# Attention plus gated MLP on one core: head quads outside, query chunks inside, and an exp on VectorE as four shifted bit lines

## The chip, the cores and the metric

The kernel runs on one core of a Trainium2 chip. The metric is the time of one execution in device microseconds (us). Both kernels were run several times on the same chip in alternation, and every run quoted here as a comparison is of the state "fast" unless the text says otherwise. The engines are TensorE (PE in the profile, PEld for its weight loads), VectorE (DVE), ScalarE (ACT), GpSimd (POOL) and SyncE (SP, which issues most DMA). The "granted clock" is the share of full speed that TensorE was given; in the mean of 0.859 of the kernel before, 294 of its 1038 us ran at 0.5 and the others at 1.0 (the first 26 us have no record).

## The reference

For x of 2048 x 640, in bf16:

```python
g = sigmoid((x * gate_w).sum(-1))            # one gate per token
q, k, v = split(x @ wqkv)                    # 32 heads of 20
a = softmax(q @ k.T * 20**-0.5) @ v @ wo     # full attention, no mask
h = x @ w1 + b1                              # 640 -> 1536
b = (h * tanh(log1p(exp(h)))) @ w2           # mish, 1536 -> 640
out = g * a + (1 - g) * b
```

The cost is dominated by softmax. There are 32 heads x 2048 x 2048 scores, 134 million exps. The kernel computes scores transposed: a block is 128 keys (partitions) x 512 queries of one head. A *group* is four heads with one chunk of 512 queries. There are 32 groups, each with 16 key tiles x 4 heads = 64 blocks, 2048 blocks in all.

## The kernel before

Four engines work on a block. TensorE makes the scores of four heads in four row strips of its array (contraction 20, padded to 32). ScalarE takes three or two blocks per activation out of the score banks and writes exp to bf16. TensorE multiplies with V in four column strips ("PV"), accumulating 32 columns per head in one PSUM bank, where the 21st is the softmax denominator. Some key tiles go to VectorE instead, which builds exp by hand. A small list scheduler inside the kernel fixes the instruction order of each engine when the program is built.

```python
DVE_KEYS = (6, 10, 14)            # 3 of 16 key tiles on VectorE, 13 on ScalarE
...
def ex(...):                      # ScalarE: one exp over 3 or 2 blocks
    nc.scalar.activation(eb.tile[:, 0:w], sb.tile[:, 0:w], ACT.Exp, bias=lnc, scale=inv)
...
# VectorE: bits of 2**y as a line, then power of two, mantissa, square, product
nc.vector.tensor_scalar(out=vb_.tile[...], in0=db.tile, scalar1=P * LOG2E * inv,
                        scalar2=127.0 * P, op0=ALU.mult, op1=ALU.add)       # x4, one per head
nc.vector.tensor_scalar(out=nb_.tile, in0=vb_.tile, scalar1=0xFF80, ... bitwise_and)
nc.vector.tensor_scalar(out=mb_.tile, in0=vb_.tile, scalar1=0x7F, scalar2=0x3F80, ... and, or)
nc.vector.tensor_tensor(out=m, in0=m, in1=m, op=ALU.mult)                   # x2 halves
nc.vector.tensor_tensor(out=m, in0=m, in1=e, op=ALU.mult)                   # x2 halves
pv_four(G, j, 1, ...); pv_four(G, j, 0, ...); pv_four(G, j, 2, ...)         # three V copies, one per coefficient
...
for i, func in enumerate((ACT.Exp, ACT.Ln, ACT.Tanh)):                      # mish, on ScalarE
    ...
ld_wk0 = load(nc.sync, ...); ld_wq0 = load(nc.scalar, ...)                  # small weights first
for c in range(4): ld_x.append(load((nc.sync, nc.scalar)[c % 2], ...))      # then x
ld_wv = load(nc.scalar, ...); ld_gw = load(nc.scalar, ...)                  # on ScalarE's queue too
```

The projections and the MLP use the whole 128 x 128 array (full mode). The group order is query chunk outside, four heads inside, so the output projection of a chunk can run as soon as its eight groups are done.

The softmax here doesn't subtract the row's maximum and nothing guards it: scores larger than these inputs give would overflow.

## Time and profile before

| | before |
|---|---|
| time, median (lowest to highest) of 4 runs | 1041.86 us (1031.25 to 1044.37) |
| span of the profiled run | 1038.2 us |
| ScalarE busy | 921.6 us (89%) |
| TensorE / VectorE busy | 831.3 / 790.8 us |
| mean granted clock of TensorE | 0.859 |
| first exp starts / last exp ends | 27.4 / 1015.5 us |

The profile page gives the busy time of each engine (part 1) and the span in 40 slices (part 2, where 9 means 90% or more):

```profile
PE 831.3 (80%) x6247; PEld 267.3 (26%) x6304; DVE 790.8 (76%) x1322; ACT 921.6 (89%) x731; POOL 35.3 (3%) x29
...
ACT  1757879998999999999999999999999999999991
...
PEclk9998999886696779997789989787989997599766
```

ScalarE is full from about the seventh slice to the last but one. The page's groups, costliest first (busy us, mean ns of one | idle before them and who ended it):

```profile
L597 ACT ACTIVATE E<-S,lnc 128x1536 bf16<-128x1536 f32 (+1 forms) x666 | 822.4, 1357 | 72.5 <-PE C L507 41.9
L579 PE MATMUL S<-q,kt_all 32*128 32x512 bf16 x1664 | 290.5, 428 | 146.1 <-ACT E L597 139.7
...
L663 DVE TENSOR_TENSOR m<-m 128x1024 bf16<-128x1024 bf16 x192 | 127.2, 683 | 0.3
...
L658 DVE TENSOR_SCALAR m<-e 128x2048 uint16<-128x2048 uint16 x96 | 66.2, 690 | 6.6 <-PE C L507 4.0
```

The exps take 822.4 us, 1.235 us each, and wait only 72.5. TensorE waits 139.7 us for ScalarE to free the score banks. So ScalarE bounds the kernel. The last two lines matter for the change: one VectorE operation with a constant does 2048 columns in 690 ns, one with two tensors only 1024 columns in 683 ns.

Who waited for whom (us in total, times, longest us):

```profile
PE S L579 <- ACT E L597: 139.7, 179, 6.2
...
ACT E L597 <- PE C L507: 41.9, 19, 16.1
...
ACT L382 <- DMA w2k<-in_gate_w_dram: 19.2, 1, 19.2
```

The chain of work that ended last, as shares of the span:

```profile
ACT 49%; PE 28%; issue 11%; DVE 7%; DMA 4%; SPq 1%; ACTq 0%; DVEq 0%
```

### The profile page before, as it was taken

The page shows a single profiled execution, that of the slowest core. Times are in us where ns is not written, and L with a number is a line of the kernel's source. Part 1 is how long each engine was busy: PE and PEld are TensorE (multiplying, and loading weights), DVE is VectorE, ACT ScalarE, POOL GpSimd, SP SyncE. Part 2 cuts the span into 40 slices and gives each one's busy share as a digit, 9 for nine tenths or more (in the row PEclk, how much of TensorE's full clock was granted, in tenths as well). Part 3 has the DMA queues.
Part 4 walks back from the last instruction along what each step waited for, and adds up shares of the span by engine and source line. Part 5 has one row for each costly group of instructions (what it writes and reads, how often), then busy time and mean ns, then how long its engine had stood idle before and what let it go on. Part 6 is the DMA issues. An engine that isn't in the chain of part 4 may idle for free.

```text
span 1038.2 us, 15472 instructions
## 1 busy us (share of the span) xinstructions
PE 831.3 (80%) x6247; PEld 267.3 (26%) x6304; DVE 790.8 (76%) x1322; ACT 921.6 (89%) x731; POOL 35.3 (3%) x29
## 2 busy tenths in 40 slices
PE   2899988887886589996689889667988967798885
PEld 1432222221121123321123322112322311132213
DVE  1698989887784769995679879677888975689772
ACT  1757879998999999999999999999999999999991
POOL 9300000000000000000000000000000000000000
PEclk9998999886696779997789989787989997599766
DMA  7400000011000000000000000000000000000001
GB/s 196 109 1 12 12 11 11 12 55 36 9 12 11 11 1 12 25 24 12 11 1 12 18 25 18 12 12 1 12 12 25 24 12 11 1 12 12 11 11 37
DMA packets 28495, 22.36 MB, mean 22 GB/s; under 512 B 15496, under 2 KB 23688, under 8 KB 28424
## 3 DMA queue, kind: packets, MB, share of 16 engines
q1 hardware_dynamic: 24744, 19.15, 6.7%
q10 hardware_dynamic: 3680, 2.23, 0.8%
q8 instruction: 49, 0.80, 0.3%
q14 instruction: 22, 0.18, 0.1%
HBM read 18.22 MB, written 2.88 MB: 20 GB/s over the span
## 4 chain that ended last, share of the span: by engine, by line
ACT 49%; PE 28%; issue 11%; DVE 7%; DMA 4%; SPq 1%; ACTq 0%; DVEq 0%
ACT E L597 40%; PE S L579 8%; PE C L507 7%; ACT arena L745 6%; PE X L763 3%; PE X L778 3%; PE X L427 2%; DVE e L646 2%; ACT L745 2%; PE X L439 2%; DMA rbc<-rows 2%; PE X L462 2%; PE X L727 1%; DMA w2k<-in_A_wqkv_dram 1%; ACT L597 1%
## 5 line engine op out<-in xcount | busy, mean ns | idle before, releaser
L597 ACT ACTIVATE E<-S,lnc 128x1536 bf16<-128x1536 f32 (+1 forms) x666 | 822.4, 1357 | 72.5 <-PE C L507 41.9
L579 PE MATMUL S<-q,kt_all 32*128 32x512 bf16 x1664 | 290.5, 428 | 146.1 <-ACT E L597 139.7
L646 DVE TENSOR_SCALAR e<-X 128x512 uint16<-128x512 f32 x384 | 260.8, 687 | 135.7 <-PE X L634 131.8
L507 PE MATMUL C<-E,va 128*32 128x512 bf16 x1664 | 183.3, 438 | 2.7 <-DVE oraw L690 1.5
L579 PEld LDWEIGHTS <-kt_all 32*128 32x128 bf16 x1664 | 83.4, 92 | 382.7 <-issue 375.6
L634 PE MATMUL X<-q,kt_all 32*128 32x512 bf16 x384 | 156.1, 428 | 3.6 <-DVE e L646 3.3
L663 DVE TENSOR_TENSOR m<-m 128x1024 bf16<-128x1024 bf16 x192 | 127.2, 683 | 0.3
L668 DVE TENSOR_TENSOR m<-m,e 128x1024 bf16<-128x1024 bf16 x192 | 126.6, 681 | 0.0
L507 PEld LDWEIGHTS <-va 128*32 128x32 bf16 x1664 | 42.5, 95 | 129.4 <-issue 127.4
L727 PE MATMUL X<-xt,w 128*128 128x512 bf16 x219 | 70.5, 416 | 2.5 <-issue 1.7
L658 DVE TENSOR_SCALAR m<-e 128x2048 uint16<-128x2048 uint16 x96 | 66.2, 690 | 6.6 <-PE C L507 4.0
L763 PE MATMUL X<-w2k,arena 128*128 128x320 bf16 x384 | 69.6, 305 | 0.7 <-DVE e L646 0.7
L745 ACT ACTIVATE arena<-arena 128x2048 bf16<-128x2048 bf16 x36 | 68.2, 1917 | 0.2
L653 DVE TENSOR_SCALAR n<-e 128x2048 uint16<-128x2048 uint16 x96 | 65.8, 685 | 0.0
L778 PE MATMUL X<-wo,arena 128*128 128x320 bf16 x256 | 49.3, 325 | 7.8 <-DVE arena L717 6.5
L507 PE MATMUL C<-e,vd 128*32 128x512 bf16 x384 | 49.5, 442 | 4.1 <-DVE e L646 2.2
L507 PE MATMUL C<-m,vd 128*32 128x512 bf16 x384 | 49.1, 452 | 4.2 <-DVE m L668 4.2
L439 PE MATMUL X<-xt,wq 128*128 128x512 bf16 x137 | 48.6, 446 | 2.3 <-issue 1.8
L733 DVE TENSOR_SCALAR arena<-X,b 128x512 bf16<-128x512 f32 x48 | 35.8, 746 | 18.7 <-PE X L727 18.5
L507 PEld LDWEIGHTS <-vd 128*32 128x32 bf16 x1152 | 34.6, 99 | 57.7 <-issue 51.6
L507 PE MATMUL C<-n,vd 128*32 128x512 bf16 x384 | 42.7, 432 | 5.7 <-DVE n L653 5.5
L427 PE MATMUL X<-xt,w2k 128*128 128x512 bf16 x147 | 44.2, 403 | 2.4 <-issue 1.1
(55 smaller groups left out, 435.7 us busy)
## 6 DMA issues: line engine op xcount, KB each, us to landing
rbc<-rows SPq DMA_DIRECT2D x128, 64.0 KB
out_dram<-arena SPq DMA_DIRECT2D x16, 160.0 KB
w<-in_B_w_dram SPq DMA_DIRECT2D x1, 1920.0 KB
w2k<-in_B_w_dram SPq DMA_DIRECT2D x1, 1920.0 KB
arena<-in_A_wqkv_dram SPq DMA_DIRECT2D x2, 700.0 KB
arena<-in_A_x_dram ACTq DMA_DIRECT2D x2, 640.0 KB
arena<-in_A_x_dram SPq DMA_DIRECT2D x2, 640.0 KB
wo<-in_A_wo_dram SPq DMA_DIRECT2D x4, 200.0 KB
```

The costliest lines, as they stand in the source:

```text
L439: nc.tensor.matmul(t[:, 0:QC], lhsT=wq[:, p, k, :], rhs=xt[:, qc, k, :], start=a, stop=b)
L507: nc.tensor.matmul(acc[32 * r:32 * r + 32, :], lhsT=ten[:, off:off + 32], rhs=srcs[r](), start=k == 0, stop=k == pv_per - 1, tile_position ...
L579: nc.tensor.matmul(sb.tile[:, a * QC:(a + 1) * QC], lhsT=kt_all[32 * r:32 * r + 32, G % NP, j * P:(j + 1) * P], rhs=q_buf[G].tile[32 * r:3 ...
L597: nc.scalar.activation(eb.tile[:, 0:w], sb.tile[:, 0:w], ACT.Exp, bias=lnc, scale=inv)
L634: nc.tensor.matmul(db.tile[:, :], lhsT=kt_all[32 * r:32 * r + 32, G % NP, j * P:(j + 1) * P], rhs=q_buf[G].tile[32 * r:32 * r + 32, :], st ...
L646: nc.vector.tensor_scalar(out=vb_.tile[:, r * QC:(r + 1) * QC], in0=db.tile[:, :], scalar1=P * LOG2E * inv, scalar2=127.0 * P, op0=ALU.mul ...
L663: nc.vector.tensor_tensor(out=m, in0=m, in1=m, op=ALU.mult)
L668: nc.vector.tensor_tensor(out=m, in0=m, in1=e, op=ALU.mult)
L727: nc.tensor.matmul(t[:, 0:QC], lhsT=w1[:, k, ft * P:(ft + 1) * P], rhs=xt[:, c, k, :], start=a, stop=b)
L745: nc.scalar.activation(v, hs[:, 4 * a:4 * a + 4, :] if func == ACT.Exp else v, func, bias=1.0 if func == ACT.Ln else 0.0)
L763: nc.tensor.matmul(t[:, 0:320], lhsT=hs[:, k, u * P:(u + 1) * P], rhs=w2[:, k, 320 * hf:320 * hf + 320], start=a, stop=b)
L778: nc.tensor.matmul(t[:, 0:320], lhsT=otn[:, (c * NP + k) % NO, u * P:(u + 1) * P], rhs=wo[:, k, 320 * hf:320 * hf + 320], start=a, stop=b)
```

## The change

The change rewrites the body of the kernel. Its parts, with the lines that carry them:

```diff
-DVE_KEYS = (6, 10, 14)                      # 3 of 16 key tiles on VectorE
+SHIFTS = (0, 19, 51, 90); SUM = 5.2566
+def dve_keys(G): n = 4; ...                 # 4 of 16
 ...
-opn (and), opm (and, or), sq x2, p3 x2; V copies for three coefficients
+nc.vector.tensor_scalar(out=bufs[i].tile[...], in0=bufs[0].tile[...],
+                        scalar1=float(SHIFTS[i]), scalar2=None, op0=ALU.add)   # i = 1, 2, 3
+# PV: the four lines are summed by TensorE with the same V
 ...
-qc, p = divmod(G, NP)                       # query chunk outside
+p, qc = divmod(G, NQ)                       # head quad outside
 ...
-nc.tensor.matmul(t[:, 0:QC], lhsT=w1[:, k, ft * P:(ft + 1) * P], rhs=..., ...)
+for r in range(4):                          # projections, MLP: four column strips
+    nc.tensor.matmul(t[32 * r:32 * r + 32, 0:width], lhsT=lhsT(r), rhs=rhs, ...,
+                     tile_position=(0, 32 * r))
 ...
+if i == 1 and a == 0:
+    nc.scalar.preload_act_table_set("natural_log_exp_and_others")  # exp and ln in one set
 ...
-x after the small weights; padding of weights by GpSimd; wv and gate_w on ScalarE's queue
+x first; no padding; wv and gate_w on SyncE's queue
 ...
+place(): four DMA copies per group pack the heads into 120- and 80-row tiles (6 steps, not 8)
```

The scores times 128 log2(e) plus 127 x 128, stored as an integer and read as bf16, give a piecewise linear picture of exp. The sum of four such lines with shifted bits is smoother, and the common factor 5.2566 goes into ScalarE's exps as a bias. Both schedulers try to let VectorE's score matmuls ride in the unused row strips of ScalarE's score passes. In the traces (matmuls that start within 0.06 us of each other counted as one step) 331 of 384 ride so in the kernel before. The changed kernel begins with 20 matmuls on TensorE whose result is thrown away.

Intent: less work for ScalarE, paid with a cheaper exp on VectorE and some more PV on TensorE.

## The prediction

> **What bounds it now.** ScalarE. On the page of before (span 1038.2 us) ScalarE is busy 921.6 (89%), TensorE 831.3, VectorE 790.8. In the 900-1000 us window ScalarE is busy 96.4 with 80 exps (1.21 us each; groups: 1571 and 1144 ns by form, overlapping their neighbours). Sum: 666 exps x 1.22 = 813 us, 36 mish activations 68, 25 table loads x 1.28 = 32, waits before exps 72.5, start (first exp at 27.4 us), tail 22.7 after the last exp. Of the waits, 23.8 are three stalls on PV matmuls before 110 us.
>
> **What the change does.**
> 1. VectorE takes 4 of 16 key tiles instead of 3; ScalarE keeps 1536 score blocks of 1664: 615 exps instead of 666 (instruction order). 51 x 1.22 = -62 us.
> 2. Table loads fall from 25 to 9: -20 us (1.28 us each here, no visible pause around them).
> 3. VectorE: before, a batch of four blocks is 4x687 + 690 + 685 + 4x682 = 6.85 us; after, 4x687 + 3x690 = 4.82, as the shifts have the form of the 690 ns operation. [...] 128 batches cost 617 us against 658. Starts stand 0.60 apart for 0.69 recorded, so VectorE needs about 730-770 us in all.
> 4. TensorE: PV groups rise from 704 to 896 (x 0.23 = +44 us); output projection from 256 to 192 steps (-9). Row visits stay about 620, but mode switches fall from 1496 to 1290. [...] group starts are 0.23 apart within a mode, 0.32-0.33 across. So -206 x 0.1 = -20 us. Net +15: about 700 us at full clock, an estimate, 780-800 at the granted 0.86.
> 5. GpSimd's padding goes; x loads before weights. First exp near 15 us instead of 27; early stalls shrink by about 10. Tail: one more copy (+2.5), fewer steps (-2).
>
> **Critical path.** Nearly all of 1, 2 and 5 lies on ScalarE's chain: -62 -20 -12 -10 = -104. TensorE and VectorE come close: per group of four heads and 512 queries I estimate ScalarE 26, TensorE 25, VectorE 23 us, so a few more waits, with four exp buffers instead of five.
> Sum: start 15 + early stalls 15 + exps 750 + mish 68 + loads 12 + other waits 45 + tail 24 = 929.
>
> **Predicted: 930 us**, range 890 to 985. Faster by over 2%: 0.92; within: 0.05; slower: 0.03.
>
> **What would show it.** Groups: 615 exps, about 760 us busy; ScalarE above 88%; shifts near 690 ns, VectorE about 770 us; windows: exps every 1.22 us in the middle; first exp near 15 us; PV step still 0.23; granted clock 0.86 or higher [...].
>
> **What would make it wrong.** Column tiles of 320 columns must be issued as eight instructions in 0.14 us; no trace here shows such a rate (PV: eight in 0.23). [...] The fixed instruction order may stall ScalarE where real times differ; output projections all fall into the last groups and may lengthen the end. If VectorE's score waits feed back through the two shared X banks, gaps reach 80 us.

The sum came to 929 us. The costs it uses are those of the trace of the kernel before: 690 ns for a VectorE operation with a constant on 2048 columns, 683 ns for one with two tensors on 1024, 0.23 us from one PV group to the next and 0.32 to 0.33 across a mode switch. The 0.14 us for a step of 320 columns is measured there too: at full clock its full-array matmuls of 320 columns start 0.14 to 0.15 us apart (448 of them).

## The result, and the profile after

The changed kernel took 943.79 us (median of 4 runs, 942.05 to 946.2), against 1041.86 us. The ratio is 0.9078, 95% interval 0.9011 to 0.9145. (Ratios here are the mean time of one kernel's fast runs over that of the other's of the same rounds, so not quite the ratio of the medians.) The prediction was 930 with a range of 890 to 985.

The page of the changed kernel, parts 1, 2 and 4:

```profile
PE 854.3 (91%) x10616; PEld 306.1 (33%) x10616; DVE 755.0 (80%) x1225; ACT 842.2 (89%) x663; POOL 5.5 (1%) x7
...
PEclk9999986699999975999999669999985799867997
...
PE 59%; ACT 22%; DVE 11%; issue 5%; DMA 2%; SPq 1%; ACTq 0%; DVEq 0%
```

The chain has gone over from ScalarE (49% to 22%) to TensorE (28% to 59%), and TensorE is busy 91% of the span. Read alone, this says that TensorE is the bound now. The experiments below ask whether that is so. The groups:

```profile
L627 ACT ACTIVATE E<-S,lnc 128x1536 bf16<-128x1536 f32 x615 | 767.1, 1332 | 63.4 <-PE C L588 40.9
L661 DVE TENSOR_SCALAR t<-X 128x512 uint16<-128x512 f32 x512 | 346.8, 688 | 108.5 <-PE X L600 99.5
L600 PE MATMUL S<-q,kt 20*128 20x512 bf16 x1536 | 259.3, 414 | 43.8 <-ACT E L627 40.6
L674 DVE TENSOR_SCALAR t<-t 128x2048 uint16<-128x2048 uint16 x384 | 252.4, 683 | 3.5 <-PE C L588 1.6
```

There are 615 exps instead of 666, and TensorE waits 40.6 us for ScalarE where it waited 139.7. The sum over ScalarE, from the two groups tables and the order of its instructions in time:

| piece of ScalarE's line | before | after | difference |
|---|---|---|---|
| until the first exp | 27.4 | 11.9 | -15.5 |
| exps, busy | 822.4 | 767.1 | -55.3 |
| table loads (25, 9) x 1.283 | 32.1 | 11.5 | -20.5 |
| mish activations | 68.2 | 69.0 | +0.8 |
| waits just before exps | 72.5 | 63.4 | -9.1 |
| from the last exp to the end | 22.7 | 27.4 | +4.7 |

The differences add up to -94.9 us; the spans differ by 96.4 us (1038.2 to 941.8). The pieces overlap by a few us (the first exp's wait is in two rows, neighbouring groups overlap), which is what is left.

The end got longer. The changed kernel's last 30 us in order of time (start, duration, what, idle before):

```profile
908.83 5.56 ACT L627 ACTIVATE E<-S,lnc 128x1536 bf16<-128x1536 f32 x5 [0.22 <-PE C L588]
...
915.21 5.82 PE L407 MATMUL X<-wo,oc 120*32 120x320 bf16 x164
...
925.07 0.69 DVE L732 TENSOR_TENSOR on<-oraw,rbc 128x512 bf16<-128x512 f32 x1 [4.13 <-DMA rbc<-rows]
925.79 3.05 SPq L741 DMA_DIRECT2D oc<-on  x4
930.15 7.93 PE L407 MATMUL X<-wo,oc 80*32 80x320 bf16 x172 [9.12 <-DMA oc<-on]
```

The denominators travel through DMA as before, then come four new copies (925.79 to 930.15, 4.4 us), then 43 steps of output projection. The line of 915.21 also answers a doubt of the prediction: 164 matmuls are 41 steps of four column strips, 5.82 / 41 = 0.142 us a step at full clock (1.00 from 915.2 to 921.1 us). Four narrow matmuls of 320 columns with their weight loads are issued in that time, which is the rate that the prediction had seen in no trace.

### The profile page after: what moved, and what is told of

Same layout as the page of the kernel before. It is cut to its first block, busy times and chain, and to the rows that moved or that the text cites. A ratio compares the mean times of both kernels' runs of the same rounds, so it can differ in the third digit from the quotient of the medians.

```text
span 941.8 us, 24292 instructions
## 1 busy us (share of the span) xinstructions
PE 854.3 (91%) x10616; PEld 306.1 (33%) x10616; DVE 755.0 (80%) x1225; ACT 842.2 (89%) x663; POOL 5.5 (1%) x7
## 3 DMA queue, kind: packets, MB, share of 16 engines
q8 instruction: 83, 1.36, 0.6%
## 4 chain that ended last, share of the span: by engine, by line
PE 59%; ACT 22%; DVE 11%; issue 5%; DMA 2%; SPq 1%; ACTq 0%; DVEq 0%
ACT E L627 20%; PE C L588 18%; PE S L600 15%; PE X L407 13%; DVE t L661 5%; PE X L600 4%; PE X L479 3%; PE X L462 3%; PE X L498 2%; DVE t L674 2%; ACT arena L771 1%; DMA rbc<-rows 1%; DVE arena L757 1%; SPq L727 1%; DVE on L732 1%
## 5 line engine op out<-in xcount | busy, mean ns | idle before, releaser
L627 ACT ACTIVATE E<-S,lnc 128x1536 bf16<-128x1536 f32 x615 | 767.1, 1332 | 63.4 <-PE C L588 40.9
L661 DVE TENSOR_SCALAR t<-X 128x512 uint16<-128x512 f32 x512 | 346.8, 688 | 108.5 <-PE X L600 99.5
L600 PE MATMUL S<-q,kt 20*128 20x512 bf16 x1536 | 259.3, 414 | 43.8 <-ACT E L627 40.6
L674 DVE TENSOR_SCALAR t<-t 128x2048 uint16<-128x2048 uint16 x384 | 252.4, 683 | 3.5 <-PE C L588 1.6
L588 PE MATMUL C<-t,va 128*32 128x512 bf16 x2048 | 208.1, 421 | 8.1 <-DVE t L674 4.7
L600 PE MATMUL X<-q,kt 20*128 20x512 bf16 x512 | 200.8, 413 | 5.8 <-DVE t L661 4.1
L600 PEld LDWEIGHTS <-kt 20*128 20x128 bf16 x2048 | 79.0, 92 | 295.3 <-issue 286.2
L407 PE MATMUL X<-w,arena 128*32 128x320 bf16 x1536 | 78.9, 308 | 3.3 <-DVE t L661 2.5
L407 PE MATMUL X<-xt,w 128*32 128x512 bf16 x960 | 76.2, 383 | 4.3 <-DVE arena L757 1.9
L479 PE MATMUL X<-xt,wqk 128*32 128x512 bf16 x560 | 49.5, 429 | 0.5 <-DVE t L661 0.5
L462 PE MATMUL X<-xt,wqk 128*32 128x512 bf16 x560 | 44.5, 402 | 0.5 <-DVE t L661 0.5
```

What stands on the lines that cost most here:

```text
L407: nc.tensor.matmul(t[32 * r:32 * r + 32, 0:width], lhsT=lhsT(r), rhs=rhs, start=a, stop=b, tile_position=(0, 32 * r))
L462: nc.tensor.matmul(t[32 * r:32 * r + 32, 0:QC], lhsT=w, rhs=xt[:, sc, k, :], start=k == 0, stop=k == KT - 1, tile_position=(0, 32 * r))
L479: nc.tensor.matmul(t[32 * r:32 * r + 32, 0:QC], lhsT=w, rhs=xt[:, qc, k, :], start=k == 0, stop=k == KT - 1, tile_position=(0, 32 * r))
L588: nc.tensor.matmul(acc[G][32 * r:32 * r + 32, :], lhsT=va4[:, (p // 2) % 2, j, h * VW:h * VW + 32], rhs=buf.tile.bitcast(BF16)[:, off * QC ...
L600: nc.tensor.matmul(t[:, off * QC:(off + 1) * QC], lhsT=kt[32 * r:32 * r + DH, (p % 2) * S + j * P:(p % 2) * S + (j + 1) * P], rhs=q_buf[G] ...
L627: nc.scalar.activation(eb.tile[:, 0:w * QC], sb.tile[:, 0:w * QC], ACT.Exp, bias=lnc, scale=inv)
```

## The experiments

Twelve kernels ran, four to a chip. The kernel before was run on each of the chips (medians 1038.5, 1040.6 and 1040.4 us). The changed kernel itself was not run again there, so differences to its 943.8 us carry the difference between chips, which for the kernel before is 0.3%. In the table, the clock is the range of mean granted clocks over the fast runs; the medians count every run, also one slow run of keys3 and three of best, the ratios only fast ones.

| run | what | time, us (median) | ratio to before, 95% | clock |
|---|---|---|---|---|
| (changed) | | 943.79 | 0.9078 [0.9011, 0.9145] | 0.887-0.900 |
| keys3 | 3 key tiles on VectorE | 1009.70 | 0.9690 [0.9598, 0.9782] | 0.822-0.837 |
| keys5 | 5 key tiles | 1132.73 | 1.0904 [1.0831, 1.0977] | 0.817-0.836 |
| pvless | TensorE -59 us, rescheduled | 966.21 | 0.9293 [0.9238, 0.9348] | 0.831-0.840 |
| pvsame | TensorE -59 us, same order | 956.22 | 0.9196 [0.9167, 0.9224] | 0.835-0.843 |
| htwice | TensorE +52 us | 955.98 | 0.9189 [0.9138, 0.9241] | 0.925-0.937 |
| oldcost | VectorE's exp at the old cost | 1214.02 | 1.1658 [1.1636, 1.1680] | 0.755-0.761 |
| fullmode | MLP, output projection in full mode | 939.28 | 0.9025 [0.8981, 0.9068] | 0.898-0.915 |
| spread | mish spread in time | 947.19 | 0.9114 [0.9077, 0.9152] | 0.892-0.905 |
| tail | shorter end | 936.99 | 0.9011 [0.8977, 0.9045] | 0.885-0.908 |
| best | fullmode + spread + tail | 970.03 | 0.9232 [0.9182, 0.9283] | 0.869-0.879 |
| tablesonly | kernel before + one table set | 1014.27 | 0.9753 [0.9715, 0.9792] | 0.856-0.867 |
| xfirst | kernel before + x first | 1035.09 | 0.9960 [0.9909, 1.0011] | 0.860-0.869 |

Theory S says that ScalarE's line of exps still bounds the kernel. The rival, theory T, says that TensorE does, as the chain and its 91% suggest.

### keys3 and keys5: move key tiles between ScalarE and VectorE

```diff
 def dve_keys(G):
-    n = 4
+    n = 3        # keys3;  n = 5 in keys5
```

> The changed kernel with 3 of 16 key tiles on VectorE instead of 4: 666 exps on ScalarE instead of 615, 800 PV groups instead of 896. Theory S (ScalarE's chain bounds): 51 exps x 1.247 us (767.1 busy over 615) = +64, a little back from waits: 985 to 1005 us. Theory T (TensorE, 91% busy, bounds now): 96 PV groups x 0.23 less, so 920 to 945 us.

> The changed kernel with 5 of 16 key tiles on VectorE: 563 exps (-52 x 1.247 = -65 us of ScalarE), 96 PV groups more (+22 us of TensorE at full clock), 32 more batches on VectorE (32 x (4 x 0.605 + 3 x 0.61) = +136 us, so about 890 busy). Theory S alone: 880 to 900 us. If VectorE or TensorE is the next limit close behind: 945 to 990 us, with ScalarE's busy share down to about 80%.

The run keys3 took 1006.9 us in the mean of its three fast runs (the median above counts a slow one of 1021 us too), 63 us more, although TensorE had 96 PV groups less to do. That is just above the range of theory S (985 to 1005), and against theory T, which had it faster. The clock fell too (0.835 for 0.893 in the profiled runs), so it could be a rival cause. The sum over ScalarE leaves no room for it. The page of keys3:

```profile
PE 863.9 (86%) x10232; PEld 298.1 (30%) x10232; DVE 622.3 (62%) x1001; ACT 905.7 (90%) x714; POOL 5.5 (1%) x7
...
L627 ACT ACTIVATE E<-S,lnc 128x1536 bf16<-128x1536 f32 (+1 forms) x666 | 831.0, 1335 | 64.2 <-PE C L588 39.1
```

ScalarE's busy time rose by 63.5 us (842.2 to 905.7), its waits before exps stayed (63.4 and 64.2), and the span rose by 62.2 (941.8 to 1004.0).

The run keys5 took 1132.7 us, slower than the kernel before, and far past both expectations. ScalarE needed only 711.0 us for its 563 exps, but waited; the same line of the waits, first for the changed kernel, then for keys5:

```profile
ACT E L627 <- PE C L588: 40.9, 52, 3.9
```

```profile
ACT E L627 <- PE C L588: 220.5, 115, 10.8
```

An exp that waits for PV waits for one of the four buffers that PV has to free. VectorE was busy only 889 us (78%), TensorE 1030 us (91%). A first reading is that the PV matmuls stand in a fixed order on TensorE, the bit lines among them, so that everything behind stands still when VectorE's lines come late. TensorE's own waits speak against that as the whole cause. The longest that it spent on VectorE's exp in keys5:

```profile
PE X L600 <- DVE t L661: 11.5, 43, 0.5
PE C L588 <- DVE t L674: 7.5, 12, 2.6
```

All such waits come to about 32 us (19 in the changed kernel). A rival is that TensorE has more to do: only 150 of VectorE's 640 score matmuls ride with ScalarE's, so that all scores take 1074 steps instead of 826. At the 0.23 us of a step at full clock that is 57 us more, an estimate, on top of 22 us of PV. The lower clock (0.828) is not the whole cause either: at full clock too ScalarE was idle for 159 of 710 us, against 34 of 711 in the changed kernel (from the first exp to the last, by the trace's clock records). None of this was tested by itself, so why keys5 lost 190 us stays open.

### oldcost: the fourth tile with the old exp's cost

```diff
-    nc.vector.tensor_scalar(out=t_i, in0=t0, scalar1=SHIFTS[i], op0=ALU.add)
+    for _ in range(2):       # the same operation twice: same result
+        nc.vector.tensor_scalar(out=t_i, in0=t0, scalar1=SHIFTS[i], op0=ALU.add)
```

> Each of the three shift operations on VectorE is done twice, which leaves the result right and gives a batch of four blocks 4 x 0.687 + 6 x 0.683 = 6.85 us, what the old exp cost. VectorE: 755 + 128 x 3 x 0.61 = 989 us busy. If the cheap exp is what makes the fourth key tile affordable: VectorE becomes the bound, 1030 to 1080 us, no better than the kernel before. If VectorE has room for it: below 980 us.

It took 1214 us: in this design the fourth key tile is affordable only because the exp became cheap. The size was again missed by more than 130 us, in the same way as in keys5: VectorE was busy 1008.5 us (83%), as expected, and the exps waited 264.5 us for PV. Here too few of VectorE's score matmuls ride (160 of 512). Both runs say that this design does not degrade gently when VectorE gets more to do.

### pvless, pvsame and htwice: take work from TensorE, or add some

```diff
 # pvless, pvsame: PV of two of the four bit lines is not issued (wrong result on purpose)
-    for items in d_items[G]:
-        pv_four(G, items)
+    for i, items in enumerate(d_items[G]):
+        pv_four(G, items, skip=i % 4 > 1)     # pvsame: the scheduler still counts 228 ns
 # htwice: the first MLP matmul is done twice, the sum starting anew
-    KT, 219, mm,
+    2 * KT, 219, mm,                           # k = k % KT
```

> Wrong result on purpose: the PV matmuls of two of the four bit lines are left out, VectorE still makes all four. TensorE loses 256 groups x 0.23 = 59 us at full clock, ScalarE and VectorE lose nothing. Theory S: only part of the 57 us of waits on TensorE goes, 915 to 935 us. Theory T: 885 to 900 us.

> The first MLP matmul is done twice (the accumulation starts anew, the result is right): 240 column groups more, +52 us of TensorE at full clock, nothing more on ScalarE or VectorE. Theory S: TensorE has some room, 950 to 970 us. Theory T: the whole cost shows, 995 us or more.

> Wrong result on purpose, as pvless (two of four bit lines are not multiplied with V), but with every other TensorE instruction in exactly the order of the changed kernel (9592 of 9592 in place), as the scheduler is told the old cost. The run pvless took 59 us of work from TensorE and came out slower (966 us, clock 0.836). Theory O (the other order that the scheduler chose was to blame): 915 to 940 us, clock about 0.89. Theory C (TensorE's granted clock follows its own activity, so work taken away is paid back as half clock): clock 0.80 to 0.86, 945 to 970 us.

Theory C of pvsame is a guess, drawn from the clocks of pvless (0.836) and htwice (0.925) against 0.893 in the changed kernel. The run pvless was expected to be faster than the changed kernel under both theories, and was 22 us slower. Its clock had fallen from 0.89 to 0.84, and the scheduler had also chosen another order, so pvsame was made to tell the two apart: the order of the remaining 9592 matmuls was exactly that of the changed kernel. It took 956 us, 12 us more than the changed kernel with 59 us of TensorE work less (256 groups x 0.23, an estimate), at a clock of 0.84. So the other order may account for the further 10 us of pvless's loss, not for all of it. The intervals of the ratios of pvsame and of the changed kernel lie close (0.9167 to 0.9224, and 0.9011 to 0.9145), but do not overlap, and the clocks are far apart. In the other direction, htwice (ordered anew) added 52 us of work (240 column groups, an estimate; two such groups take 0.44 us, from 129.26 to 129.70, in the changed kernel), cost 12 us, which lies in the range of theory S, and its clock went up to 0.93.

Where the time went is seen by stages. First the changed kernel, then pvsame, in three windows: length; busy us (instructions) of PE, PEld, DVE, ACT, POOL; granted clock; DMA share and rate:

```profile
200.00:300.00 100.00, 95.69 (x1357) 35.08 (x1354) 87.98 (x144) 95.80 (x79) 0.00 (x0) 1.00 0.07 16
...
700.00:800.00 100.00, 88.98 (x1130) 30.23 (x1123) 76.36 (x122) 94.89 (x75) 0.00 (x0) 0.82 0.06 15
800.00:900.00 100.00, 89.60 (x1013) 28.29 (x1010) 79.80 (x134) 90.80 (x73) 0.00 (x0) 0.83 0.08 21
```

```profile
200.00:300.00 100.00, 93.03 (x1259) 33.26 (x1258) 86.93 (x142) 95.12 (x78) 0.00 (x0) 0.98 0.06 16
...
700.00:800.00 100.00, 85.28 (x980) 27.17 (x977) 76.41 (x123) 95.53 (x74) 0.00 (x0) 0.78 0.05 12
800.00:900.00 100.00, 91.47 (x783) 23.98 (x781) 71.61 (x117) 81.79 (x66) 0.00 (x0) 0.61 0.07 20
```

In the stage at full or nearly full clock (200 to 300 us) both do the same number of activations, 79 and 78, so the TensorE work that pvsame leaves out is worth nothing there: ScalarE is the limit. By 900 us pvsame is 13 activations behind. It lost seven of them in the last of these windows, where its clock is 0.61 instead of 0.83 and ScalarE does 66 instead of 73, and four before 100 us, where its clock was lower too (0.91 for 0.98 from 25 to 100 us).

The sum over all stretches says the same. From the first exp to the last, by the trace's clock records, ScalarE was idle for 34 of 711 us at full clock and 29 of 191 us at half clock in the changed kernel, and for 28 of 612 and 52 of 307 us in pvsame. So pvsame's profiled span, longer by 17.7 us (959.5 for 941.8), has 23 us more of idle ScalarE at half clock and 6 us less at full clock. At full clock the share of idle time is the same (4.8% and 4.5%) with and without the 59 us of TensorE work, so ScalarE is the limit there, which is theory S; but with little to spare, for in htwice it was idle for 50 of 783 us (6.4%). At half clock TensorE more often makes it wait, which is theory T, though not throughout. In this stretch of the changed kernel ScalarE was full, with mish and exps, and TensorE was not:

```profile
167.00:177.00 10.00, 6.67 (x58) 1.95 (x62) 6.82 (x10) 9.99 (x8) 0.00 (x0) 0.54 0.02 2
```

The clock records of the traces hold only 1.0 and 0.5, in stretches that are, but for the ends, multiples of 3.41 us: at half clock from 3.41 to 27.31 us long in the changed kernel and in the kernel before (202 us of the span at half clock in the changed kernel, 294 in the kernel before, 317 in pvsame). No record stands before 9 us in the changed kernel, and before 26 us in the kernel before; the mean clocks count that time as full. With 59 us less TensorE work the clock was lower (pvsame, 0.84 for 0.89), with 52 us more it was higher (htwice, 0.93). But it was also halved without an idle TensorE. This is the changed kernel around one loss of the clock:

```profile
122.00:129.00 7.00, 6.51 (x89) 2.16 (x85) 6.23 (x11) 6.82 (x6) 0.00 (x0) 1.00 0.01 4
129.00:136.00 7.00, 5.76 (x66) 2.40 (x64) 6.65 (x11) 7.00 (x6) 0.00 (x0) 0.95 0.01 1
136.00:143.00 7.00, 6.76 (x49) 1.42 (x46) 4.04 (x9) 5.41 (x4) 0.00 (x0) 0.50 0.17 41
143.00:150.00 7.00, 6.60 (x39) 1.48 (x35) 3.88 (x7) 6.08 (x5) 0.00 (x0) 0.50 0.05 12
```

TensorE was busy 5.76 of 7 us before it lost half its clock, and 6.76 of 7 after, with fewer instructions (49 and 39, for 66). No wait of TensorE in 129 to 136 us was longer than 0.71 us.

That time goes with the clock is also seen without any edit: within one and the same kernel the slower runs mostly had the lower clock. In fullmode the four runs were 934.0, 938.3, 940.3 and 945.4 us at 0.915, 0.907, 0.905 and 0.898; in pvless and htwice, with four runs each, time and clock have a correlation of -0.97. It is negative in every kernel run here, but from -0.60 to -0.99, and the slope is no constant: about 7 us per 0.01 of clock in fullmode (11.3 us over 0.017), 2.4 in tail. A correlation doesn't tell what drives what. The edit of pvsame changed TensorE's work alone, and both clock and time moved.

Nor does the amount of work alone set the clock: keys5, with 22 us more of it (96 groups x 0.23, an estimate), had a lower clock as well (0.817 to 0.836), and oldcost, with the same matmuls, the lowest (0.755 to 0.761). Both spread the work over a longer time (1132.7 and 1214.0 us).

### spread: is it the crowding of mish that costs the clock?

ScalarE's mish operations come in bursts, in which TensorE gets fewer score banks to fill (24 exps in the 49.4 us from 128.6 to 178.0 of the changed kernel, 79 in the 100 us from 200 to 300). In the four stretches of the changed kernel with mish (128.6 to 178.0, 315.8 to 363.6, 498.3 to 544.5 and 682.4 to 732.1 us) the granted clock was 0.65, 0.75, 0.82 and 0.70, against 0.893 over the span. The guess, theory C below, was that spreading them would keep the clock up.

```diff
-    after=at(group + 0.45 * i + 0.12 * a)
+    after=at(group + (1.2 + 0.9 * a, 1.5 + 0.9 * a, 3.5 + 0.5 * a)[i])   # exp, ln, tanh
-    mish(c, base + 3.1)
+    mish(c, base)
```

> The changed kernel with the nine mish activations of each chunk spread over 3.3 groups instead of 1.4 (exp and ln between the softmax exps, tanh later), nothing else. Theory C (half clock comes where mish crowds out the exps and TensorE runs thin): granted clock 0.91 to 0.95 instead of 0.89, waits of the exps down, 930 to 940 us. If the half clock has another cause: clock 0.88 to 0.90, 940 to 950 us.

The clock stayed at 0.892 to 0.905 and the time at 947.2 us. The guess fell. (The edit also shifted the second MLP matmul a little, 4.8 + 1.8 for 4.6 + 2.0 in the code, so "nothing else" is not quite so.) What exactly makes the clock drop stays open.

### fullmode: undo the column tiles of MLP and output projection

```diff
-    for r in range(4):
-        nc.tensor.matmul(t[32 * r:32 * r + 32, 0:width], lhsT=lhsT(r), rhs=rhs, ..., tile_position=(0, 32 * r))
+    nc.tensor.matmul(t[:, 0:width], lhsT=lhsT, rhs=rhs, ...)    # and mode="full" for the scheduler
```

> Undoes the column tiles of the MLP and the output projection alone: each step is one 128-wide matmul in full mode. TensorE's mode switches rise from 1290 to 1447, at 0.1 us each +16 us of TensorE; 2448 fewer matmuls. Theory S: mostly hidden, 943 to 955 us. Theory T: 955 to 970 us. If issuing four narrow matmuls costs time that one wide one does not, it comes out faster, below 940 us.

939.3 us, ratio 0.9025 [0.8981, 0.9068] against 0.9078 [0.9011, 0.9145] of the changed kernel: no loss, perhaps a small gain. (The median lies just under the 940 us of the third expectation, but the runs reach from 934 to 945.) The column tiles of these parts brought nothing, though 157 mode switches came back (1290 to 1447). The prediction had costed the fewer switches at 0.1 us each. A switch does cost that on TensorE; a stretch of the kernel before shows it:

```profile
500.43 0.40 PE L507 MATMUL C<-E,va 128*32 128x512 bf16 x4
500.66 0.39 PE L507 MATMUL C<-n,vd 128*32 128x512 bf16 x4
501.00 0.40 PE L579 MATMUL S<-q,kt_all 32*128 32x512 bf16 x3
...
501.33 0.40 PE L507 MATMUL C<-E,va 128*32 128x512 bf16 x4
```

Starts are 0.23 us apart within the column mode, and 0.34 and 0.33 where column strips give way to row strips and back. But 16 us of that (157 x 0.1, an estimate), in the engine that is not the limit in the full-clock stages, did not show in the time. Some of it may be hidden, as the run also has 2448 matmuls fewer and a slightly higher clock (0.898 to 0.915, for 0.887 to 0.900). Loads of 128x32 weights take 95 to 102 ns in the profiles of the kernel before and of the changed one, those of 128x128 weights 97 to 110 (147 for the first twenty of the changed kernel).

### tablesonly and xfirst: two parts alone, in the kernel before

```diff
 # tablesonly
+    if func == ACT.Ln and a == 0:
+        nc.scalar.preload_act_table_set("natural_log_exp_and_others")
 # xfirst: in the order of the changed kernel
+    x0a = load_x(nc.scalar, 0, 2); x0b = load_x(nc.sync, 2, 4)
     ld_wk0 = ...; ld_wq0 = ...
```

> The kernel before with one part of the change alone: the table set that has exp and ln both is loaded ahead of ln, so that 9 table loads are left of 25. 16 x 1.28 = 20.5 us less on ScalarE. Theory S: ratio 0.98 to the kernel before, 1015 to 1025 us. If these loads stood in ScalarE's slack: within 1% of before.

> The kernel before with one part of the change alone: the loads of x go ahead of the small weight loads, in the changed kernel's order. First exp near 13 us instead of 27.4. If the start is worth what the prediction said: 10 to 15 us off. If the next obstacle (GpSimd's fills of the V buffers end only near 30 us) takes it back: 2 to 8 us off.

The table loads were worth 26 us alone (ratio 0.9753; by its interval 22 to 30 us), a little more than 16 x 1.283 = 20.5 us. That is 1.6 us for each load left out; the waits just before the 24 later loads of the kernel before sum to only 0.5 us in its groups.

The run xfirst gained nothing clear (ratio 0.996, interval up to 1.0011). The first exp came at 27.8 us, as before. x was there earlier: transposes ran from 4.96 us. Then they stopped:

```profile
4.96 1.89 PE L363 MATMUL S<-ident,arena 128*128 128x128 bf16 x16 [4.96 <-DMA arena<-in_A_x_dram]
21.15 0.59 PE L363 MATMUL S<-ident,arena 128*128 128x128 bf16 x4 [14.30 <-ACT xt L380]
```

They waited for a copy on ScalarE, and ScalarE (the same run) was still busy issuing DMA:

```profile
2.40 0.53 ACTq L288 DMA_DIRECT2D w2k<-in_A_wqkv_dram  x1
13.53 0.37 ACTq L288 DMA_DIRECT2D w2k<-in_gate_w_dram  x1
18.38 0.38 ACTq L288 DMA_DIRECT2D w2k<-in_A_wqkv_dram  x1
18.79 1.28 ACT L380 ACT_TABLE_LOAD   x1 [18.79 <-DMA w2k<-in_gate_w_dram]
```

Its fourth load was issued at 2.40, its fifth only at 13.53 and its sixth at 18.38 us, and only then could it compute. This is the wait of 19.2 us in the profile of before. The changed kernel has no such loads on ScalarE's queue: only three, issued by 2.4 us, and its first copy runs at 7.04 us, its first exp at 11.94. There was a second obstacle. VectorE pads the first weights of k and q, and these landed only at 17.1 us:

```profile
17.12 0.36 DVE L326 COPY w2k<-arena 128x400 bf16<-128x400 bf16 x1 [15.57 <-DMA arena<-in_A_wqkv_dram]
```

(The obstacle named in the expectation: in the trace of the kernel before, GpSimd fills the V buffers until 25.3 us, and ends its last fill at 29.5.) So x first alone gains nothing clear. The start of the changed kernel has the later loads off ScalarE's queue and no padding as well. (Neither was run alone, nor with x first, in the kernel before; why the fifth issue was held so long is not shown either, only that it was.)

### tail and best: what the readings suggest

```diff
 # tail
+    wo7: the rows of wo for the last four heads, padded to the layout of the normalised tile
+    f_last(): for 8 output tiles in the banks X0, X1, S1, S0, C
+        steps k = 0..4 as soon as the last PV is read out
+        step 5 from the normalised tile itself, without the four copies
```

> The changed kernel with another end: the last chunk's output projection does five of its six steps while the last normalisation is under way, in the score and PV banks that are free by then, and the sixth reads the normalised tile itself, without the four copies. The 27.4 us from the last exp to the end should become 18 to 21 us: 934 to 938 us, clock as before.

> The three edits that should not hurt together: MLP and output projection in full mode (939 us alone), mish spread, the shorter end. If they add up: 920 to 930 us.

The run tail took 936.99 us with runs of 932.7 to 939.1, all below the lowest of the changed kernel (942.05). The last exp ends at 917.8 and the span at 937.3, so 19.5 us instead of 27.4. The adds of the last chunk (seven of eight shown) now follow each other:

```profile
929.37 0.69 DVE L735 TENSOR_TENSOR on<-oraw,rbc 128x512 bf16<-128x512 f32 x1 [1.70 <-DMA rbc<-rows]
930.49 1.01 DVE L867 SCALAR_TENSOR_TENSOR arena<-X,g,w 128x320 bf16<-128x320 f32 x2 [0.43 <-PE X L408]
931.41 2.37 DVE L867 SCALAR_TENSOR_TENSOR arena<-S,g,w 128x320 bf16<-128x320 f32 x5
```

By its median it is the fastest kernel of this study, 0.7% below the changed one and 10% below the kernel before; fullmode, with an interval that overlaps, is not clearly slower.

The run best should have been faster still (920 to 930 us), and is slower: its four fast runs took 956 to 970 us, 962 in the mean. Three more were slow (980 to 986), and the median of all seven is 970. Its clock is 0.869 to 0.879 in the fast runs, lower than that of any of its three parts. Each part alone was harmless; together they gave the scheduler another order, with 1485 mode switches. Whether the order or the clock is to blame was not told apart. (The 1485, like the other counts of switches, comes out of the trace too, from the order of the weight loads.)

One more idea, a fifth exp buffer, was built but not run, and the kernel before with a fourth key tile at the old exp was not run; oldcost stands for it.

## Why the prediction was right, point by point

The time (943.8 for 930) and the direction were right.

- **What bounds it.** ScalarE in the kernel before (tablesonly: 20.5 us less on it, 26 us gained), and in the changed kernel where the clock is full (keys3: +63 us, where 51 exps x 1.247 = 64). The prediction named TensorE as close; at half clock it makes ScalarE wait (29 of 191 us).
- **Step 1, exps.** 615 exps as foretold. The mis-sized term is the cost of one: 1.22 us, read in a window without waits, where 767.1 / 615 = 1.247 is what an exp costs over the whole run. (Where no mish and few waits stand between them it still was 1.21: 79 exps in 95.80 us busy, from 200 to 300 us.) 615 x 0.027 = 17 us, which is more than the 14 us by which the total was missed. The mean over all exps of the kernel before (822.4 / 666 = 1.235) would have been nearer.
- **Step 2, table loads.** 9 loads, -20.5 us, as foretold, and shown alone by tablesonly (-26).
- **Step 3, VectorE.** The shift takes 683 ns (690 foretold) and VectorE is busy 755 us (730 to 770). The run oldcost shows that this is what the fourth tile hangs on.
- **Step 4, TensorE.** PV steps and the 0.142 us of the 320-column steps agree; eight instructions in 0.14 us, which no trace had shown, are issued. The -20 us for fewer mode switches is not seen in the time (fullmode). The busy time was 854.3 us for 780 to 800: the page counts modelled, overlapping durations (PV: 421 ns for a matmul, where groups of four start 0.23 us apart), so an estimate in starts is not comparable with it. Its rise of 23.0 us (831.3 to 854.3) is nearer to the +15 foretold.
- **Step 5, start and end.** First exp at 11.9 us for 15. Of the two reasons given, x before weights failed as a cause by itself (xfirst), and the padding was not tested. The early stalls did shrink by 10 us: the waits before exps up to 110 us went from 29.9 to 19.9. The end was to stay the same and grew by 4.7 us; the copy that was put at 2.5 us took 4.4.
- **Idle time.** Start 15, early stalls 15, other waits 45 and tail 24 make 99; measured, 941.8 - 842.2 = 99.6. The sum is right, partly by luck, as the start was shorter and the end longer.
- **The clock.** The changed kernel's clock is higher (0.89 for 0.86; foretold 0.86 or higher), and pvsame, with less TensorE work than the changed kernel, has a lower one than it (0.84). The sum had no term for the clock, and why it rose is not shown.

## What to carry to other kernels

Before cutting work on an engine that looks busy, ask by stages what it limits: here 59 us less of TensorE work made the kernel 12 us slower, and the granted clock went down with it (0.89 to 0.84). Moving work to another engine paid here only up to a point; one step further (a fifth key tile, or the old exp's cost) lost 190 to 270 us, far more than the engine's busy time would tell; what exactly was lost there stays open. And the first and last 30 us are worth reading line by line: an engine that was held by its own DMA issues, and score banks that stood idle during the last normalisation, were found there and in no total.
